# Splitting block 0's state product in a linear-attention plus gated-FFN kernel: two halves between gate and value of units 1 and 4, one decayed k on VectorE, plain idle products

## Chip, cores and metric

The kernel runs on one core of a Trainium2 chip. The metric is the device time of one execution in microseconds (us); lower is better. Kernels that are compared ran on the same chip in interleaved rounds. Engines are named as in the profile: PE is TensorE, DVE is VectorE ("Vector"), ACT is ScalarE ("Scalar"), POOL is GpSimd. PSUM, in the prediction, is where the kernel puts TensorE's results (its `psum()` tiles); XT is the attention output as the FFN reads it.

## The reference

Decayed linear attention over blocks, whose output goes through a gated FFN. Sizes: 4 batches, 8 heads, 768 positions, head dimension 64; FFN 512 to 1536 to 512.

```python
# for each block of positions, per head (lam is the decay of the head):
intra    = ((q @ k.T) * Dmask) @ v              # Dmask[i, j] = lam ** (i - j) for i >= j
inter    = (q * lam ** (pos + 1)) @ kv_state
out      = intra + inter
kv_state = lam ** block * kv_state + (k * lam ** (block - 1 - pos)).T @ v
# then, on x = out as (3072, 512):
y = (sigmoid(x @ w_gate) * (x @ w_val)) @ w_out
```

The kernel takes 128 positions at a time, so there are six blocks, numbered 0 to 5. "Decayed k" is the factor `k * lam ** (...)`; the "state product" is decayed k times v. A "unit" is a group of 128 of the 1536 FFN columns: four products of gate, a sigmoid on Scalar, four products of value, and one multiplication ("product") of the two on Vector.

## The kernel before

Weights and q, k, v are loaded by GpSimd's own DMA queue, so GpSimd spends time on issuing every load (0.76 to 1.17 us each in its timeline below), in program order with its arithmetic.

```python
WG, WV                                     # weights of gate and value, loaded in pieces:
def load_w(t, src, i, w):                  #   every load is issued by GpSimd
    nc.gpsimd.dma_start(out=t[:, :, fs], in_=src[:, :, fs])
# ...
zero = const.tile([128, 2 * C], FP32, tag="zero")           # C = 128
def idle(n):                                                # keeps TensorE busy while it waits
    for i in range(n):
        nc.tensor.matmul(wm[:, :2 * C], lhsT=zero[:, :C], rhs=zero, start=True, stop=True, ...)
# ...
def make_lamq():                                            # powers of lam for blocks 1 to 5
    lp = const.tile([128, HP, C], FP32, tag="lp")
    for u in range(2):
        us = slice(u * 64, (u + 1) * 64)
        nc.vector.tensor_copy(lp[us]..., lam_bc[us, :]...)              # 64 x 4, one input
    w = 1
    while w < C:                                                        # seven doublings, two inputs
        nc.vector.tensor_tensor(out=lp[:, :, w:2 * w], in0=lp[:, :, 0:w], in1=..., op=ALU.mult)
        w *= 2
    nc.vector.tensor_copy(lamq, lp)                                     # 128 x 512, one input
# ...
def make_kd(n):
    if n == 0:
        for bp in range(NB2):                               # two halves, two batches each
            nc.gpsimd.tensor_tensor(out=KD[n][:, bs], in0=K[n][:, bs], in1=kds..., op=ALU.mult)
        return
# ...
def c(n, *pairs):                                           # state product: 16 products per half,
    for bp in pairs:                                        # then Vector copies it to Sb
        ...
# ... order of the program around block 0:
piece_m(0, 3)                              # last mask product on Vector
# ...
prod(0, 0, v0)                             # unit 0
load_gv(3, GW)                             # GpSimd: issue two weight loads
make_kd(0)                                 # GpSimd: decayed k, both halves
load_gv(4, GW)                             # GpSimd: two weight loads
load(1, "qk", 0, 2)                        # GpSimd: q and k of block 1
# ...
gv(0, 1)                                   # unit 1: gate, sigmoid, value, product
make_lamq()
for ft in (2, 3): ...                      # gates 2 and 3
for ft in (2, 3): ...                      # values 2 and 3, products 2 and 3
gv(0, 4)                                   # unit 4
c(0, 0, 1)                                 # state product, both halves
# ...
gv(0, 5, 6, 7)
```

## Time and profile before

| | before |
|---|---|
| time, first three runs | 227.41 us median (227.41 to 227.60) |
| span that the profile records | 225.6 us |
| TensorE busy | 218.8 us, 97% |
| gate 1 / value 1 / gate 2 start | 16.95 / 18.32 / 19.34 us |
| value 4 / state product / gate 5 start | 24.00 / 24.96 / 25.59 us |

The engine table and the row of granted clock on the page of the kernel before (engine, busy us, share, instructions; one digit of the clock per fortieth of the span):

```profile
PE 218.8 (97%) x1746; PEld 117.5 (52%) x1768; DVE 104.2 (46%) x191; ACT 79.1 (35%) x149; POOL 80.8 (36%) x76
PEclk9999999999999999999999999999999999999999
```

TensorE is the engine that bounds the kernel. From 26 us to the end it is busy 195.5 of 199.6 us, and its products follow each other without holes that matter, so a gain has to come from the start. There the holes are few. The chain of waits of the kernel before (start us, us, what; it is the path that ended last):

```profile
11.18 7.09 DMA WV<-in_moe_w_val_dram
18.27 0.05 issue
18.32 1.04 PE vp L429 x4
19.35 3.63 PE gp L437 x16
...
23.28 0.68 DVE ht L450
23.96 0.04 issue
24.00 1.02 PE vp L429 x4
25.03 0.63 PE cp L407 x32
```

Value 1 waits for its weights, value 4 waits for Vector's product of unit 2, and the state product stands between value 4 and gate 5. Why Vector is late is seen in its timeline before (start us, us, engine, line, operation, out<-in, shape, count, and in brackets the idle time before it):

```profile
19.46 0.69 DVE L432 TENSOR_TENSOR ht<-sg,vp 128x512 bf16<-128x512 bf16 x1 [1.22 <-PE vp L429]
20.07 0.61 DVE L181 COPY lp<-lam_bc 64x4 f32<-64x4 f32 x2
20.71 1.85 DVE L185 TENSOR_TENSOR lp<-lp 128x4 f32<-128x4 f32 x7
22.60 0.77 DVE L188 CAST lamq<-lp 128x512 bf16<-128x512 f32 x1
23.28 1.26 DVE L450 TENSOR_TENSOR ht<-sg,gp 128x512 bf16<-128x512 bf16 x2
```

After the product of unit 1 (19.46) it builds lamq, and only then multiplies units 2 and 3. GpSimd's timeline before, over the same time:

```profile
16.70 3.77 POOL L361 TENSOR_TENSOR kd<-kb,kds 128x1024 bf16<-128x1024 bf16 x2
20.40 0.80 POOL L102 DMA_DIRECT2D WG<-in_moe_w_gate_dram  x1
21.20 0.76 POOL L102 DMA_DIRECT2D WV<-in_moe_w_val_dram  x1
21.94 1.17 POOL L85 DMA_DIRECT2D qb<-in_q_dram  x1
23.09 1.17 POOL L85 DMA_DIRECT2D kb<-in_k_dram  x1
```

The first of lamq's two copies took longer than its twin, as the view of that source line shows (minimum, median and maximum ns):

```profile
L181 DVE COPY lp<-lam_bc x2: 170/299/428, 20.1 to 20.5; 64x4 f32<-64x4 f32 x2
```

The long one ended at 20.50 us, just after GpSimd's decayed k (20.46).

### The profile page before, as it was taken

Reading aid. Unit: us, or ns where it says so; the run is one execution under the profiler, and the core shown is the slowest. Engines: PE = TensorE matmul, PEld = TensorE weight load, DVE = VectorE, ACT = ScalarE, POOL = GpSimd, SP = SyncE. Lnnn points to the kernel's source line nnn. Section 1 sums busy time; section 2 is a strip of 40 time slices with the busy share of each in tenths; the row PEclk is TensorE's granted clock in tenths of the full one; section 3 lists DMA queues with packets and bytes.
Section 4 is the critical chain, followed back from the end, with each engine's and each line's share of the span. In section 5 each row is a group of like instructions: output and inputs, shape, how many; then the busy total and the mean of one; then the engine's idle time right before and its main releaser. Section 6 shows DMA issues by size and latency. Waiting matters only on the chain.

```text
span 225.6 us, 4279 instructions
## 1 busy us (share of the span) xinstructions
PE 218.8 (97%) x1746; PEld 117.5 (52%) x1768; DVE 104.2 (46%) x191; ACT 79.1 (35%) x149; POOL 80.8 (36%) x76
## 2 busy tenths in 40 slices
PE   7989999999999999999999999999999999999994
PEld 5653455788864455444446444446444445444443
DVE  7866746586530522435642345742334850333300
ACT  5554234435422225333115333225333224433221
POOL 8999967973691007940005950000000000000000
PEclk9999999999999999999999999999999999999999
DMA  6999999999999991999021999921820012100022
GB/s 111 155 172 196 188 177 156 156 191 166 157 188 171 221 175 72 217 150 122 1 96 46 145 146 148 75 94 51 188 46 0 3 46 93 49 0 0 0 94 96
DMA packets 105860, 25.72 MB, mean 114 GB/s; under 512 B 95984, under 2 KB 102896, under 8 KB 105840
## 3 DMA queue, kind: packets, MB, share of 16 engines
q0 software_dynamic: 81232, 13.90, 79.7%
q1 hardware_dynamic: 23568, 11.28, 20.8%
q10 hardware_dynamic: 1040, 0.26, 0.5%
q8 instruction: 14, 0.23, 0.4%
q14 instruction: 6, 0.05, 0.1%
HBM read 28.32 MB, written 6.29 MB: 153 GB/s over the span
## 4 chain that ended last, share of the span: by engine, by line
PE 90%; POOL 4%; DMA 3%; issue 1%; DVE 0%; DVEq 0%; POOLq 0%
PE po L486 27%; PE vp L429 21%; PE gp L423 21%; PE gp L458 5%; PE vp L464 5%; DMA WV<-in_moe_w_val_dram 3%; PE sp L302 2%; PE gp L437 2%; PE op L314 2%; POOL vb L96 2%; PE op L326 1%; PE cp L407 1%; PE po L475 1%; POOL kb L96 1%; POOL qb L96 1%
## 5 line engine op out<-in xcount | busy, mean ns | idle before, releaser
L432 DVE TENSOR_TENSOR ht<-sg,vp 128x512 bf16<-128x512 bf16 x56 | 38.5, 687 | 66.8 <-PE vp L429 62.7
L486 PE MATMUL po<-WO,ht 128*128 128x512 bf16 x266 | 61.3, 379 | 0.5
L423 PE MATMUL gp<-XT,WG 128*128 128x512 bf16 x217 | 57.2, 379 | 0.6
L429 PE MATMUL vp<-XT,WV 128*128 128x512 bf16 x220 | 56.6, 379 | 0.5 <-DMA WV<-in_moe_w_val_dram 0.3
L426 ACT ACTIVATE sg<-gp 128x512 bf16<-128x512 f32 x56 | 33.4, 597 | 62.6 <-PE gp L423 62.6
L486 PEld LDWEIGHTS <-ht 128*128 128x128 bf16 x276 | 26.3, 98 | 31.0
L429 PEld LDWEIGHTS <-WV 128*128 128x128 bf16 x224 | 21.8, 98 | 27.4 <-DMA WV<-in_moe_w_val_dram 0.8
L423 PEld LDWEIGHTS <-WG 128*128 128x128 bf16 x224 | 21.4, 98 | 25.3
L489 ACT COPY ob<-po 128x512 f32<-128x512 f32 x23 | 13.5, 585 | 52.3 <-PE po L486 48.4
L199 DVE TENSOR_TENSOR MT<-sp,mask 128x512 bf16<-128x512 f32 x40 | 25.1, 682 | 10.3 <-PE sp L302 10.3
L388 POOL TENSOR_TENSOR sd<-Sb,dec 128x512 f32<-128x512 bf16 x8 | 8.1, 1035 | 43.8 <-DVE Sb L414 43.8
L458 PE MATMUL gp<-XT,WG 128*128 128x256 bf16 x96 | 14.4, 273 | 0.0
L464 PE MATMUL vp<-XT,WV 128*128 128x256 bf16 x96 | 14.4, 273 | 0.0
L468 DVE TENSOR_TENSOR ht<-sg,vp 128x256 bf16<-128x256 bf16 x24 | 10.0, 420 | 8.6 <-PE vp L464 8.6
L461 ACT ACTIVATE sg<-gp 128x256 bf16<-128x256 f32 x24 | 9.2, 383 | 13.0 <-PE gp L458 11.9
L96 POOL DMA_DIRECT2D vb<-in_v_dram x10 | 12.8, 1282 | 1.4 <-DMA kb<-in_k_dram 1.1
L379 POOL TENSOR_TENSOR kd<-kb,kds 128x1024 bf16<-128x1024 bf16 x6 | 11.3, 1903 | 3.1 <-DMA kb<-in_k_dram 3.1
L414 DVE TENSOR_TENSOR Sb<-cp,sd 128x512 bf16<-128x512 f32 x8 | 5.1, 686 | 15.5 <-PE cp L407 15.5
L341 ACT CAST XT<-op 128x512 bf16<-128x512 f32 x19 | 9.9, 598 | 2.1 <-PE op L314 2.0
L458 PEld LDWEIGHTS <-WG 128*128 128x128 bf16 x96 | 9.2, 98 | 1.7 <-issue 0.2
L464 PEld LDWEIGHTS <-WV 128*128 128x128 bf16 x96 | 9.4, 98 | 1.1
L217 PE MATMUL wm<-zero 128*128 128x256 f32 x20 | 8.4, 556 | 1.2 <-DVE ip L124 1.2
(83 smaller groups left out, 159.4 us busy)
## 6 DMA issues: line engine op xcount, KB each, us to landing
out_dram<-ob SPq DMA_DIRECT2D x21, 256.0 KB, 2.2
kb<-in_k_dram POOLq DMA_DIRECT2D x11, 256.0 KB, 10.2
qb<-in_q_dram POOLq DMA_DIRECT2D x9, 256.0 KB, 9.0
vb<-in_v_dram POOLq DMA_DIRECT2D x4, 512.0 KB, 14.1
WO<-in_moe_w_out_dram POOLq DMA_DIRECT2D x3, 512.0 KB, 8.5
WG<-in_moe_w_gate_dram POOLq DMA_DIRECT2D x5, 256.0 KB, 8.4
WV<-in_moe_w_val_dram POOLq DMA_DIRECT2D x5, 256.0 KB, 9.1
qb<-in_q_dram POOLq DMA_DIRECT2D x4, 128.0 KB, 8.3
```

What stands on the lines that cost most here:

```text
L96: nc.gpsimd.dma_start(out=lst[n][:, b0:b1], in_=src[b0:b1, :, sl, :].rearrange("b h s d -> s (b h) d"))
L199: nc.vector.tensor_tensor(out=out.rearrange("p (e x) c -> p e x c", e=2), in0=x.rearrange("p (e x) c -> p e x c", e=2), in1=mask.rearrange ...
L379: nc.gpsimd.tensor_tensor(out=KD[n][:, e], in0=K[n][:, e], in1=kds[:, e::2].unsqueeze(1).unsqueeze(3).to_broadcast([128, B, HP, D]), op=AL ...
L423: nc.tensor.matmul(gp, lhsT=WG[:, mt, fs], rhs=x[:, mt, :], start=(mt == 0), stop=(mt == NMT - 1))
L426: nc.scalar.activation(sg, gp, AF.Sigmoid)
L429: nc.tensor.matmul(vp, lhsT=WV[:, mt, fs], rhs=x[:, mt, :], start=(mt == 0), stop=(mt == NMT - 1))
L432: nc.vector.tensor_mul(HT[n, ft], sg, vp)
L458: nc.tensor.matmul(gp[:, cs], lhsT=WG[:, mt, fs], rhs=x[:, mt, cs], start=(mt == 0), stop=(mt == NMT - 1))
L464: nc.tensor.matmul(vp[:, cs], lhsT=WV[:, mt, fs], rhs=x[:, mt, cs], start=(mt == 0), stop=(mt == NMT - 1))
L468: nc.vector.tensor_mul(HT[n, ft][:, cs], sg[:, cs], vp[:, cs])
L486: nc.tensor.matmul(po, lhsT=HT[n, ft][:, tt * 128:(tt + 1) * 128], rhs=WO[:, ft, :], start=(ft == 0), stop=(ft == NFT - 1))
L489: nc.scalar.copy(ob, po)
```

## The change

The intent is to put half of the state product into the hole before value 1, so that less stands between value 4 and gate 5. For that, the first half of decayed k must be ready sooner, so it goes to Vector, which is idle then (1.25 us before 15.95 in the profile before). The idle products become bf16 of 512 columns in place of fp32 of 256. The diff, cut to its core:

```diff
-    zero = const.tile([128, 2 * C], FP32, tag="zero")
+    zero = const.tile([128, TCH], BF16, tag="zero")
...
-            nc.tensor.matmul(wm[:, :2 * C], lhsT=zero[:, :C], rhs=zero, start=True, stop=True,
+            nc.tensor.matmul(wm, lhsT=zero[:, :C], rhs=zero, start=True, stop=True,
...
+    def make_kd0(bp, eng):
+        ...                                      # one half, on the engine given
     def make_kd(n):
-        if n == 0:
-            ...                                  # both halves on GpSimd
...
-    idle(5)
+    idle(10)                                     # later counts: 1,1,1,1,1 -> 1,1,0,2,2
...
     piece_m(0, 3)
+    make_kd0(0, nc.vector)
...
     load_gv(3, GW)
-    make_kd(0)
+    make_kd0(1, nc.gpsimd)
     load_gv(4, GW)
...
-    gv(0, 1)
+    g1 = psum(); mm_part(g1, WG, 0, 1, 0, TCH); sigm(0, 1, g1)      # (joined into lines here)
+    c(0, 0)
+    v1 = psum(); mm_part(v1, WV, 0, 1, 0, TCH); prod(0, 1, v1)
     make_lamq()
...
-    gv(0, 4)
-    c(0, 0, 1)
+    g4 = psum(); mm_part(g4, WG, 0, 4, 0, TCH); sigm(0, 4, g4)
+    c(0, 1)
+    v4 = psum(); mm_part(v4, WV, 0, 4, 0, TCH); prod(0, 4, v4)
```

More of the change, by code (lines that the diff above doesn't have):

```diff
@@ L354, in piece_a0 @@
                 nc.scalar.copy(XT[0][:, m0:m0 + w, b, :], op)
-    def make_kd(n):
-        if n == 0:
-            KD[n] = kdp.tile([128, B, H, D], BF16, tag="kd", name="kd")
-            for bp in range(NB2):
-                bs = slice(2 * bp, 2 * bp + 2)
-                nc.gpsimd.tensor_tensor(
-                    out=KD[n][:, bs], in0=K[n][:, bs],
-                    in1=kds.unsqueeze(1).unsqueeze(3).to_broadcast([128, 2, H, D]), op=ALU.mult)
-            return
+    def make_kd0(bp, eng):
+        if bp == 0:
+            KD[0] = kdp.tile([128, B, H, D], BF16, tag="kd", name="kd")
+        bs = slice(2 * bp, 2 * bp + 2)
+        eng.tensor_tensor(out=KD[0][:, bs], in0=K[0][:, bs],
+                          in1=kds.unsqueeze(1).unsqueeze(3).to_broadcast([128, 2, H, D]), op=ALU.mult)
+    def make_kd(n):
         if n == 1:
@@ L515 @@
     piece_tq0([2])
-    idle(1)
     piece_tq0([3])
@@ L521 @@
     piece_m(0, 3)
+    make_kd0(0, nc.vector)
     piece_a0(0)
     piece_a0(1)
-    idle(1)
+    idle(2)
     piece_a0(2)
-    idle(1)
+    idle(2)
     g0 = psum()
@@ L564, in gvh @@
             piece_gvh(n, ft, i)
-    gv(0, 1)
+    g1 = psum()
+    mm_part(g1, WG, 0, 1, 0, TCH)
+    sigm(0, 1, g1)
+    c(0, 0)
+    v1 = psum()
+    mm_part(v1, WV, 0, 1, 0, TCH)
+    prod(0, 1, v1)
     make_lamq()
@@ L576 @@
         prod(0, ft, vp)
-    gv(0, 4)
-    c(0, 0, 1)
+    g4 = psum()
+    mm_part(g4, WG, 0, 4, 0, TCH)
+    sigm(0, 4, g4)
+    c(0, 1)
+    v4 = psum()
+    mm_part(v4, WV, 0, 4, 0, TCH)
+    prod(0, 4, v4)
     fade()
```

## The prediction

> **What bounds the kernel now.** The page's engine table has TensorE busy 218.8 of 225.6 us. In the timeline of PE, from 26 us to the end products follow each other at 0.216 us per 512 columns, apart from small gaps. The change touches nothing there, so only what happens before about 25.6 us can move the time. The chain there, gate 1, value 1, gates 2 and 3, values 2 and 3, gate 4, value 4, state product, gate 5, has three holes:
> - Value 1 starts at 18.32 us, 0.5 us after gate 1 stopped streaming (17.81), held by the load of its WV columns (chain of waits: DMA from 11.18 to 18.27).
> - Gate 2 starts at 19.34 us, 0.15 us late, behind its own load.
> - Value 4 starts at 24.00 us, 0.34 us after gate 4 stopped streaming; it waits for a PSUM buffer that the Vector product of unit 2 frees (waits view: "PE vp <- DVE ht"). Vector is late because it builds lamq first (20.07 to 23.28).
> Value 4 then ends at 24.87, the state product until 25.46, and gate 5 starts at 25.59.
>
> **What the change does.**
> 1. First half of the state product (16 products: 0.28 us by the trace, plus some 0.2 us at the changes of kind) goes to 17.9-18.3 us, into the hole before value 1. Free, with no slack; the hole before gate 2 gives 0.15 us more.
> 2. Its decayed k moves to Vector. The 512-wide mask product (same kinds of operand) repeats every 0.60 us; 1024 wide I estimate 1.13 us, 14.63 to 15.76. The next Vector instruction, the second half of XT for batch 3, started at 15.95. It fits.
> 3. GpSimd's decayed k ends at about 18.6 instead of 20.46. In the trace the first 64x4 copy of lamq took 428 ns, its twin 170 ns, and it ended 35 ns after the GpSimd product. [...] Without it the lamq chain gets 0.25 us shorter: unit 2's product starts at about 23.03, unit 3's ends at about 24.3.
> 4. Second half: takes the PSUM buffer freed by unit 2 (about 23.73), runs to about 24.05. Value 4 must now wait for unit 3's product, one buffer later: it starts at about 24.35. Gate 5 follows directly, at about 25.22 instead of 25.59.
> 5. Loads behind GpSimd are issued 1.9 us earlier; no product waits for them: worth nothing.
> 6. Idle products: ten of 512 columns at half clock need 4.27 us (before: 4.64), still ending before q's first cast (5.73). All lies in slack before 18.3 us, if the clock still rises near 7 us (the spacing of transposes fell from 107 to 56 ns there[...]).
>
> **Sum.** -0.37 us, all on the critical path: 227.41 to 227.05 us. Range 226.6 to 227.6. Chances: faster by over 2% 0.01, within 2% 0.98, slower 0.01.
>
> **Right or wrong in the profile.** Value 1 still at about 18.3; first lamq copy about 170 ns; value 4 at about 24.35, waiting for Vector; no state product after it; gate 5 near 25.2.
>
> **What would make it wrong.** [...]decayed k over 1.4 us on Vector, delaying XT and gate 1; the state's Vector copy pushing unit 1's product past 19.46; other landing times of the weights.

Clauses that no trace of this case shows are cut from it, in step 3, in step 6 and in the last paragraph, and likewise from some expectations below. -0.37 us is gate 5 at 25.22 in place of 25.59. "Without it" in step 3 means without GpSimd's decayed k beside lamq's first copy; the 0.25 us are about 428 less 170 ns.

## The result and the profile after

| | before | after |
|---|---|---|
| time | 227.41 us median of 6 (227.38 to 227.60) | 227.77 us median of 6 (227.05 to 228.10) |
| recorded spans (before: its 51 runs) | 225.6 to 225.8 us | 224.9 to 226.0 us |
| time minus span, mean of the same runs | 1.81 us | 2.12 us |

The ratio is 1.001, with a 95% interval of 0.9993 to 1.0027: within 2%. A ratio here is the mean time of one kernel's fast runs over that of the other's of the same rounds, so it is not quite the ratio of the medians that are quoted.

The predicted time was 227.05 us with a range to 227.6. The median lies 0.72 us above the forecast and outside the range. Two features were not in the forecast at all: the times of the change spread over a whole microsecond, while those of the kernel before keep within 0.4, and the part of the time that lies outside the recorded span grew by 0.3 us.

The page after, same lines as before:

```profile
PE 219.2 (97%) x1764; PEld 115.3 (51%) x1764; DVE 104.9 (47%) x192; ACT 79.2 (35%) x149; POOL 79.2 (35%) x75
PEclk9799999999999999999999999999999999999999
```

The second digit of the clock shows that in this execution the clock fell back once (the clock records give half speed from 8.58 to 12.00 us). In the same execution the first k load landed at 8.01 us, against 7.30 before. The chain of waits after begins with it:

```profile
1.26 6.75 DMA kb<-in_k_dram
...
18.78 0.37 PE cp L406 x16
19.16 5.29 PE gp L436 x24
24.44 0.37 PE cp L406 x16
24.81 0.98 PE gp L436 x4
```

And Vector's timeline after, the lines of lamq:

```profile
20.84 0.34 DVE L181 COPY lp<-lam_bc 64x4 f32<-64x4 f32 x2
21.21 1.85 DVE L185 TENSOR_TENSOR lp<-lp 128x4 f32<-128x4 f32 x7
23.09 0.43 DVE L188 CAST lamq<-lp 128x512 bf16<-128x512 f32 x1
```

From 17.76 us on this execution has no hole: gate 1, half a state product, value 1, gates, values, gate 4, the second half and value 4 follow each other, and the lamq copies are short. That is the intended picture, shifted by the late start: gate 1 began at 17.76 us against 16.95, and gate 5 at 25.63 against 25.59. So this one profile says "the change works, the loads were late". With six times between 227.05 and 228.10 one profile can't be the whole account.

### The profile page after: what moved, and what is told of

Same layout as the page of the kernel before. It is cut to its first block, busy times and chain, and to the rows that moved or that the text cites. A ratio compares the mean times of both kernels' runs of the same rounds, so it can differ in the third digit from the quotient of the medians.

```text
span 225.6 us, 4294 instructions
## 1 busy us (share of the span) xinstructions
PE 219.2 (97%) x1764; PEld 115.3 (51%) x1764; DVE 104.9 (47%) x192; ACT 79.2 (35%) x149; POOL 79.2 (35%) x75
## 4 chain that ended last, share of the span: by engine, by line
PE 94%; DMA 3%; DVE 1%; issue 0%; ACT 0%; POOLq 0%
PE po L485 27%; PE gp L422 21%; PE vp L428 21%; PE gp L457 5%; PE gp L436 5%; PE vp L463 5%; PE sp L302 3%; DMA kb<-in_k_dram 3%; PE op L314 3%; PE op L326 1%; PE cp L406 1%; PE po L474 1%; DVE MT L197 1%; PE tk L244 0%; ACT XT L354 0%
## 5 line engine op out<-in xcount | busy, mean ns | idle before, releaser
L431 DVE TENSOR_TENSOR ht<-sg,vp 128x512 bf16<-128x512 bf16 x54 | 37.2, 688 | 65.4 <-PE vp L428 65.4
L422 PE MATMUL gp<-XT,WG 128*128 128x512 bf16 x216 | 55.5, 379 | 0.0
L428 PE MATMUL vp<-XT,WV 128*128 128x512 bf16 x216 | 55.4, 379 | 0.0
L425 ACT ACTIVATE sg<-gp 128x512 bf16<-128x512 f32 x54 | 32.2, 597 | 59.5 <-PE gp L422 59.5
L428 PEld LDWEIGHTS <-WV 128*128 128x128 bf16 x216 | 21.2, 98 | 25.5
L422 PEld LDWEIGHTS <-WG 128*128 128x128 bf16 x216 | 20.7, 98 | 24.8
L457 PEld LDWEIGHTS <-WG 128*128 128x128 bf16 x96 | 9.2, 98 | 1.8 <-issue 0.2
L463 PEld LDWEIGHTS <-WV 128*128 128x128 bf16 x96 | 9.4, 98 | 1.1
L77 POOL DMA_DIRECT2D qb<-in_q_dram x8 | 9.4, 1182 | 0.0
```

Of the source, the lines that this page charges most:

```text
L422: nc.tensor.matmul(gp, lhsT=WG[:, mt, fs], rhs=x[:, mt, :], start=(mt == 0), stop=(mt == NMT - 1))
L425: nc.scalar.activation(sg, gp, AF.Sigmoid)
L428: nc.tensor.matmul(vp, lhsT=WV[:, mt, fs], rhs=x[:, mt, :], start=(mt == 0), stop=(mt == NMT - 1))
L431: nc.vector.tensor_mul(HT[n, ft], sg, vp)
L457: nc.tensor.matmul(gp[:, cs], lhsT=WG[:, mt, fs], rhs=x[:, mt, cs], start=(mt == 0), stop=(mt == NMT - 1))
L463: nc.tensor.matmul(vp[:, cs], lhsT=WV[:, mt, fs], rhs=x[:, mt, cs], start=(mt == 0), stop=(mt == NMT - 1))
```

## The experiments

Theories, with the letters that the texts use:
- **L**, load issues: with less work on GpSimd, its issue of the q load moves about 1.9 us forward, from 21.94 to about 20.1 us, and lies across lamq's small copies, which it holds up.
- **C**, clock: with the new idle products the clock rises or falls at other times, and this spreads the times.
- **D**, arrival of data: the landing times of loads vary from execution to execution whatever the kernel, so the old kernel should spread too.
- **N**, length of Vector's program: the 0.3 us outside the span come with the number of instructions that Vector has in the built program. Before it is 311, after it is 313 (the traces hold 309 and 311 Vector records, the same two more): the two more belong to the decayed k on Vector.

All runs in one table. "Outside" is time minus recorded span, mean of the runs; the ratio is against the kernel before in the same rounds.

| run | what it is | Vector instr. | median us (range) | ratio, 95% interval | outside us |
|---|---|---|---|---|---|
| before_again | the kernel before | 311 | 227.41 (227.37–227.53) | 0.9998, 0.9986–1.0010 | 1.77 |
| after_again | the change | 313 | 227.80 (227.14–228.08) | 1.0009, 0.9996–1.0022 | 2.12 |
| after_third | the change | 313 | 227.79 (227.17–228.16) | 1.0010, 0.9998–1.0021 | 2.10 |
| chain_only | change, old idle products | 313 | 227.58 (227.13–227.84) | 1.0001, 0.9988–1.0014 | 2.11 |
| idle_only | before, new idle products | 311 | 227.36 (227.34–227.78) | 0.9999, 0.9987–1.0011 | 1.77 |
| kd_only | before, half of decayed k on Vector | 313 | 227.53 (227.32–228.04) | 1.0010, 0.9998–1.0023 | 2.16 |
| c_only | change, all decayed k on GpSimd | 311 | 227.67 (227.59–227.71) | 1.0010, 0.9998–1.0022 | 1.87 |
| tt_copy | change, lamq's copies with two inputs | 313 | 227.21 (227.16–227.70) | 0.9997, 0.9983–1.0010 | 2.10 |
| pool_late | change, GpSimd kept busy as before | 313 | 227.75 (227.65–227.78) | 1.0014, 1.0002–1.0027 | 2.13 |
| lamq_late | tt_copy, lamq's cast after unit 4 | 313 | 227.29 (227.14–227.52) | 0.9996, 0.9984–1.0009 | 2.16 |
| tt_all | change, copies and cast with two inputs | 313 | 227.17 (227.10–227.79) | 0.9996, 0.9984–1.0009 | 2.13 |
| before_tt | before, lamq's copies with two inputs | 311 | 227.38 (227.36–227.54) | 0.9999, 0.9987–1.0011 | 1.81 |
| before_tt2 | before, copies and cast with two inputs | 311 | 227.31 (227.29–227.41) | 0.9995, 0.9983–1.0007 | 1.79 |
| dve_plus | before, one dead memset on Vector | 312 | 228.60 (228.56–228.63) | 1.0051, 1.0039–1.0063 | 2.07 |
| dve_two | before, two dead memsets on Vector | 313 | 228.62 (228.61–228.68) | 1.0053, 1.0040–1.0066 | 2.13 |
| after_minus | change, one Vector instruction fewer | 312 | 228.15 (227.72–228.67) | 1.0029, 1.0016–1.0042 | 2.01 |
| lamq_late_minus | lamq_late, one Vector instruction fewer | 312 | 228.01 (227.69–228.60) | 1.0027, 1.0015–1.0039 | 2.03 |
| lamq_act | change, lamq's copies on Scalar, cast late | 311 | 227.00 (226.90–227.09) | 0.9981, 0.9967–0.9994 | 1.84 |

All outputs are right. Most of these differences are smaller than their intervals, so the argument rests on the profiles, on how wide each kernel spreads, and on the split of the time into span and rest.

### Is the spread the change's own? before_again, after_again, after_third

No edit: the two kernels again.

> The old kernel once more, for a second profile. Ratio 1.000, times 227.4 to 227.6. Theory C: whatever its loads do, the clock rises near 7 us and stays up. Theory D: if the loads land at 8.0 us in this profile, its time must rise by 0.5 us or so; if k never lands later than 7.3 us in this kernel, then the late loads belong to the change.

> The change as it is, once more, for a second profile and for its spread. Theory C (clock: [...]the clock falls back to half speed for 3.4 us between 8.6 and 12 us, and the first stage runs late): the times spread again over about 1 us, from 227.0 to 228.1, and whether the clock in the trace falls back decides where the profiled run lies. Theory D (loads: the first loads simply landed 0.7 us late in the profiled run, by chance): the profiled run has k at either 7.3 or 8.0 us and gate 5 moves with it, and the old kernel, whose loads vary as much, shows the same spread.

> The change as it is, for a third profile. Theory L: in the three groups of times, 227.1, 227.8 and 228.1, the first copy or the cast of lamq tells them apart: near 228.1 a copy is held (784 ns in the second profile), near 227.1 none is and the loads are early; times 227.0 to 228.1 with a median of 227.6 to 227.9.

The kernel before gave 227.37 to 227.53. The change fell again into groups. Its 18 runs in all are 227.05, .14, .15, .17, .30, .31; then 227.74, .78, .79, .80, .80, .80, .81; then 228.05, .08, .09, .10, .16. Their mean is 227.67 us. All 51 runs of the kernel before lie between 227.33 and 227.69. So D does not hold as put: the arrival of data alone doesn't spread the old kernel.

The profile of after_again fell in the slowest group (228.08 us). Its first k load landed at 7.33 us, as before, and its clock did not fall back. Vector's timeline in after_again:

```profile
20.55 0.96 DVE L181 COPY lp<-lam_bc 64x4 f32<-64x4 f32 x2
21.55 1.85 DVE L185 TENSOR_TENSOR lp<-lp 128x4 f32<-128x4 f32 x7
23.43 0.43 DVE L188 CAST lamq<-lp 128x512 bf16<-128x512 f32 x1
23.78 1.28 DVE L449 TENSOR_TENSOR ht<-sg,gp 128x512 bf16<-128x512 bf16 x2
```

GpSimd's timeline in after_again:

```profile
16.70 1.91 POOL L360 TENSOR_TENSOR kd<-kb,kds 128x1024 bf16<-128x1024 bf16 x1
...
20.18 1.16 POOL L85 DMA_DIRECT2D qb<-in_q_dram  x1
```

TensorE's timeline in after_again:

```profile
17.85 0.44 PE L406 MATMUL cp<-vb,kd 128*64 128x64 bf16 x16
18.80 1.04 PE L436 MATMUL gp<-XT,WV 128*128 128x512 bf16 x3 [0.51 <-DMA WV<-in_moe_w_val_dram]
...
24.51 0.44 PE L406 MATMUL cp<-vb,kd 128*64 128x64 bf16 x16 [0.36 <-DVE ht L449]
25.11 1.02 PE L436 MATMUL gp<-XT,WV 128*128 128x512 bf16 x4 [0.15 <-DVE ht L449]
```

The first copy took 784 ns (20.55 to 21.33) and ended when the issue of the q load ended (21.34). Here TensorE does wait for Vector, and value 4 starts at 25.11 us in place of the predicted 24.35, gate 5 at 25.97. Gate 5 decides the span: in 19 of the 20 profiles the span is 200.0 to 200.1 us longer than its start (200.6 in lamq_late_minus, which no run explains). The profile of after_third (227.81 us, the middle group) has the same wait in a smaller form: value 1 at 18.54, first copy at 20.29 in 154 ns, second copy 785 ns (20.46 to 21.24, with the issue from 20.08 to 21.25), value 4 at 24.83.

### Which part of the change? idle_only, chain_only, kd_only, c_only

idle_only is the old kernel with the new `zero`, `idle` and counts. chain_only is the rest of the change with the old ones.

> The old kernel with only the new idle products. Theory C: slower than before and spread out, 227.4 to 228.5, median about 227.9 (ratio 1.002 or more), with the clock falling back in the slow ones. Theory D: as before, 227.4 to 227.6, ratio 1.000.

> The change with the old fp32 idle products at their five old places; decayed k and the two halves of the state product as in the change. Theory C: the clock stays up from 7 us, the spread goes, and the gain that I forecast appears: 227.05 (ratio 0.9984), value 1 at 18.3, gate 5 near 25.2 us. Theory D: as the changed kernel, 227.0 to 228.1, with a spread of 1 us.

idle_only is the kernel before: 227.36 us, copies and cast as before (195 and 775 ns in its profile), gate 5 at 25.58. One of its five runs, 227.78 us with a span of 226.0, lies above every run of the kernel before and stays unexplained. Chain_only spreads like the change (227.13 to 227.84). So the idle products are not the cause, and C falls. The clock records agree: the clock rose at 7.00 us in the first profile of the kernel before and at 5.70 in before_again, with the same gate 5 (25.59 and 25.58). Chain_only's profile happened to have a late first load again (k at 7.94 us), as the first profile of the change had.

kd_only takes one part of the rest: only the engine of decayed k's first half.

```diff
     piece_m(0, 3)
+    make_kd0(0, nc.vector)
...
-    make_kd(0)
+    make_kd0(1, nc.gpsimd)
```

> The old kernel with only the first half of the decayed k on Vector: old idle products, the state product in one piece after value 4. Theory L: GpSimd's load issues move onto lamq here too, so the times spread to 228 although the state product stays where it was: 227.1 to 228.1. My forecast would have had it 0.25 us faster, 227.15. If the state product in the holes is what costs, this one stays at 227.15 to 227.5 with no spread.

It spreads from 227.32 to 228.04 us. Vector's and then GpSimd's timeline in kd_only:

```profile
20.14 1.09 DVE L181 COPY lp<-lam_bc 64x4 f32<-64x4 f32 x2
```

```profile
20.07 1.17 POOL L85 DMA_DIRECT2D qb<-in_q_dram  x1
```

The second copy took 920 ns (20.31 to 21.23), against an issue that ended at 21.24. So moving the decayed k is enough to bring the hold and the spread, without any new place for the state product.

c_only is the counterpart: both halves of decayed k stay on GpSimd.

```diff
-    make_kd0(0, nc.vector)
...
     load_gv(3, GW)
+    make_kd0(0, nc.gpsimd)
     make_kd0(1, nc.gpsimd)
```

> The change with both halves of the decayed k on GpSimd, at the old place: only the state product in two halves and the new idle products are left. Vector has as many instructions as in the old kernel. Theory N: time minus span 1.8. In the span: the load issues stand at the old times, so the copy is held until 20.5 us and lamq ends near 23.3; value 4 waits for unit 3's product until about 24.6, gate 5 about 25.45: times 227.2 to 227.5 in a narrow band. Theory P gives the same here: this run settles the state product's own share.

The spread is gone (227.59 to 227.71) and the time outside the span is back at 1.87 us, but the median, 227.67, missed its expectation of 227.2 to 227.5. TensorE's timeline in c_only says why:

```profile
18.65 0.44 PE L406 MATMUL cp<-vb,kd 128*64 128x64 bf16 x16 [0.77 <-POOL kd L360]
```

The first half waits for GpSimd, value 1 comes only at 19.03 us, and the gain is used up. The decayed k on Vector is needed for the first half to fit in its hole; this part of the change's design is right. In c_only a copy was held as well, by another load: 392 ns from 20.78 to 21.17, across the WG issue that ended at 21.20.

### Is it the load issue that holds the copies? tt_copy, pool_late

L is tested by writing the same copy in another form, with two inputs in place of one, as the maximum of a value with itself. That a load issue would not hold this form was the assumption; no run had tested it before:

```diff
-            nc.vector.tensor_copy(lp[us]..., lam_bc[us, :]...)
+            nc.vector.tensor_tensor(out=lp[us]..., in0=src, in1=src, op=ALU.max)   # src = lam_bc[us, :]...
```

> The change, with the two 64x4 copies that begin lamq written as the maximum of a value with itself: a Vector instruction with two inputs instead of one. Theory L ([...]these copies are held until GpSimd has finished issuing q's load, which the change moved from 21.9 to 20.2 us, onto the start of lamq): both take about 170 ns in every run, gate 5 comes up to 0.6 us sooner when the loads are early, and the times near 228.1 vanish: highest about 227.85, median about 227.5. Theory F (only the landing of value 1's weights, 18.3 to 18.8 us, spreads the times): nothing changes, 227.1 to 228.1, median 227.8.

Vector's timeline in tt_copy, then GpSimd's and TensorE's:

```profile
20.30 0.33 DVE L182 TENSOR_TENSOR lp<-lam_bc 64x4 f32<-64x4 f32 x2
```

```profile
20.07 1.17 POOL L85 DMA_DIRECT2D qb<-in_q_dram  x1
```

```profile
24.22 1.02 PE L437 MATMUL gp<-XT,WV 128*128 128x512 bf16 x4
25.08 1.03 PE L423 MATMUL gp<-XT,WG 128*128 128x512 bf16 x4
```

GpSimd's issue of the q load ran from 20.07 to 21.24 us in this profile, so the two instructions lie inside it and took 151 and 163 ns. The second, which began 0.39 us into the issue, is the test: in after_third a one-input copy that began 0.38 us into it took 785 ns. (The first began 0.22 us into it, and one-input copies that began so early ran free too, in after_third and in the first profile of the change; one that began 0.24 us into it was held, 920 ns in kd_only.) Value 1 was at 18.55 us, as in after_third, yet gate 5 came at 25.08 in place of 25.69. Four of five runs were 227.16 to 227.26 (one 227.70); the group at 228.1 did not appear. The mean span fell to 225.20 us, against 225.56 for the change: the hold cost 0.36 us on average. Of the 15 runs of the three versions of the change with two-input copies and unmoved tiles (tt_copy, lamq_late, tt_all) 13 have a span of 225.3 us or less, against 6 of the 18 of the change. The two others (227.70 and 227.79, span 225.6) were not profiled, so the hold is not the only thing that can put a run in the middle group.

The ends fit as well. Take from the end of each instruction that an issue held the time that it takes when free (154 to 170 ns for a copy, 427 for the cast): in all twelve profiles with such a hold it then starts 0.16 to 0.19 us before the recorded end of the issue. That is why the cast of the kernel before runs on 0.25 us past the issue.

pool_late goes the other way. The change stays whole, but GpSimd computes the first half once more into a dead tile, so that its load issues come at the old times:

```diff
+    kdx = const.tile([128, 2, H, D], BF16, tag="kdx", name="kdx")
+    nc.gpsimd.tensor_tensor(out=kdx, in0=K[0][:, 0:2], in1=kds..., op=ALU.mult)
     make_kd0(1, nc.gpsimd)
```

> The change, with GpSimd doing the first half of the decayed k once more, into a tile that nobody reads: Vector's part and the state product stay as in the change, but GpSimd issues the later loads at the old times (20.4 us on). Theory L: GpSimd's extra work makes the kernel steadier and no slower: the first copy is held until 20.46 us again (some 400 ns), lamq ends near 23.3, value 4 starts near 24.6, times 227.2 to 227.6, median about 227.35. Theory F: as the change, 227.1 to 228.1, median 227.8, for the loads of the weights up to unit 5 are issued before this.

The spread shrank to 0.13 us, as L says. The level did not go where it was expected: 227.75, with a span of 225.5 to 225.7. With the issues at their old times the copies are free (156 ns) but the cast is held again (620 ns), and outside the span it has the 2.13 us of the change in place of 1.81.

### Does the old kernel have the hold as well? before_tt, before_tt2

Step 3 of the prediction expected 0.25 us from a lamq chain that is no longer held at its first copy. before_tt tests that alone: the kernel before, with the same edit as tt_copy.

> The old kernel with only the two 64x4 copies of lamq as a maximum (two inputs). Theory L[...]: the first copy falls from 428 to about 160 ns, but the chain reaches lamq's cast 0.25 us sooner, while GpSimd issues q's load (21.9 to 23.1 us), and the cast is held until 23.1 us as before: lamq ends near 23.28 again, times as before, 227.35 to 227.6. My forecast's step 3 (taking the hold off the first copy makes lamq 0.25 us shorter) would give 227.15.

Vector's timeline in before_tt:

```profile
20.31 0.35 DVE L182 TENSOR_TENSOR lp<-lam_bc 64x4 f32<-64x4 f32 x2
...
22.57 0.78 DVE L189 CAST lamq<-lp 128x512 bf16<-128x512 f32 x1
23.27 1.26 DVE L451 TENSOR_TENSOR ht<-sg,gp 128x512 bf16<-128x512 bf16 x2
```

In this profile value 1 happened to come at 18.56 us in place of 18.32, so the copies started at 20.31 and took 172 and 164 ns. They ended at 20.66 us, only 0.02 before those of the kernel before (20.68), so lamq reached its cast no sooner: the run is no test of what 0.25 us off the copies is worth. idle_only, with the one-input copies and value 1 at 18.54, has the same times (copies 195 and 168 ns to 20.67). The product of unit 2 started at 23.27, as before (23.28).

This shows the likely reason that the old kernel is so steady. Whether value 1 comes at 18.32 or at 18.56 us, the copies end at 20.66 to 20.68, just after GpSimd's decayed k (20.45 to 20.46), and the cast ends at 23.35 to 23.36, set by the q issue. By these figures a cast that came 0.25 us sooner would have been held to the same end; that is worked out, no run shows it. pool_late, with the old issue times, has little spread too.

before_tt2 gives the cast two inputs as well.

> The old kernel with all three one-input copies of lamq, the cast too, as a maximum; nothing else of the change. Theory L: no hold is left, the cast takes about 0.65 us and lamq ends near 22.95 instead of 23.28; value 4 follows gate 4 at about 23.7; gate 5 near 25.28; times 227.05 to 227.25, without the change. [...]

It was 227.31 us, against 227.05 to 227.25 expected. The cast took 691 ns, its full two-input time (tt_all has the same 691), so the load issue no longer held it. But the two-input first copy was held until GpSimd's decayed k ended at 20.46 us: it took 408 ns. So the edit of before_tt and before_tt2 does not take the first hold away, and "no hold is left" was wrong. So in these profiles either form is held by something: the one-input copy by a load issue (784 ns in after_again) and by GpSimd's arithmetic (428 ns before), the two-input copy by the arithmetic (408 ns here), but not by the issue that it met in tt_copy (163 ns).

### The change without any hold: lamq_late, tt_all

lamq_late is tt_copy with lamq's cast moved behind the product of unit 4; tt_all is the change with all three one-input instructions of lamq given two.

> The copies as a maximum, and lamq's last cast put after unit 4's product, so that the products of units 2 and 3 no longer wait for it. Theory L: Vector no longer holds the state product's second half and value 4; Tensor streams from gate 2 to gate 5 without a hole: gate 5 at about 25.0 to 25.5 us, times 226.8 to 227.6, median about 227.2. Theory F: gate 5 moves only with value 1, median about 227.6 or more.

> The change with all three copies of lamq as a maximum. Theory L: as the run with the two copies alone, for there the cast (427 ns) was not held; 0.2 us longer at most[...]: median 227.2 to 227.4, highest about 227.8. Were the cast held in the slower runs (those at 227.7), they would come down too: highest 227.4.

Medians 227.29 and 227.17 us, mean spans 225.16 and 225.20. In both profiles the weights of value 1 landed early (17.02 and 17.06 us), value 1 began at 18.20 and 18.23, right behind the half state product, and the copies started at 19.95 and 19.97, before the q issue (20.09 and 20.10); the second ones began 0.02 and 0.04 us into it. Gate 5 came at 25.00 and 25.05 us, sooner than the 25.22 of the prediction. The chain itself was therefore not overrated. (The highest run of tt_all, 227.79, passed the 227.4 that was expected if a held cast made the slow runs; so a held cast does not explain it.)

### What is outside the span? dve_plus, dve_two, after_minus, lamq_late_minus

N was tested by adding dead instructions to the old kernel and taking one from the change.

```diff
+    dead = const.tile([128, 1], FP32, tag="dead", name="dead")      # dve_plus, in the kernel before
+    nc.vector.memset(dead, 0.0)
```

```diff
+    dead = const.tile([128, 16], FP32, tag="dead", name="dead")     # dve_two, in the kernel before
+    for i in range(2):
+        nc.vector.memset(dead[:, i:i + 1], 0.0)
```

```diff
-    p1 = const.tile([128, 1], FP32, tag="p1")                       # the two *_minus kernels
-    for lo in range(0, 128, 32):
-        nc.vector.tensor_scalar_add(p1[lo:lo + 32], loc[lo:lo + 32, 0:1], float(lo))
+    p1 = loc[:, 0:1]
+    nc.vector.tensor_scalar_add(p1[64:128], p1[64:128], 64.0)
+    nc.vector.tensor_scalar_add(p1[32:64], p1[32:64], 32.0)
+    nc.vector.tensor_scalar_add(p1[96:128], p1[96:128], 32.0)
```

> The old kernel with one dead instruction on Vector among the constants: a memset of one column that nobody reads. Theory N (one more instruction in Vector's program costs a fixed third of a microsecond outside the recorded span): span 225.6 as before, time minus span 2.1 instead of 1.8, times 227.65 to 227.9. Theory P (the extra goes with where the decayed k is computed): span and time as before, 227.35 to 227.6.

> The change with one Vector instruction less among the constants (the partition index built by three additions in place instead of four): as many as the old kernel. Theory N: time minus span falls to 1.8 and all times by 0.33 us: 226.7 to 227.8, median about 227.45. Theory P: time minus span stays 2.1, times 227.05 to 228.15, median 227.8.

> The kernel with lamq's copies as a maximum and its cast moved back, with one Vector instruction less. Theory N: 0.33 us below lamq_late: times 226.8 to 227.2, median about 226.95, faster than both kernels in every run (ratio about 0.998). Theory P: 227.1 to 227.5 as lamq_late.

> The old kernel with two dead memsets of one column on Vector, into a new 64-byte tile, so that all other tiles keep their place modulo 64 bytes. Theory N (the length of Vector's program): span 225.6 as before, first loads at 7.3 and 9.0 us as before, time minus span 2.1 instead of 1.8: times 227.65 to 227.9. If the extra went with computing the decayed k on Vector: time minus span 1.8, times 227.35 to 227.6.

For the time outside the span N held in direction, not in size. One dead memset gave 2.07 us, two gave 2.13, against 1.77 to 1.81 of the kernel before; a fixed third of a microsecond for each instruction it is not. The two kernels with one instruction fewer were expected at 1.8 because the change was taken to have one more than the kernel before. It has two, so they stand at 312, and the time outside fell by only 0.10 and 0.13 us, to 2.01 and 2.03. Over all kernels the values are 1.77 to 1.87 at 311 instructions, 2.01 to 2.07 at 312 and 2.10 to 2.16 at 313. The trace has no record outside the span, so the mechanism stays open; shown is only that the added time goes with the number of Vector's instructions. That dead ones do it rests on kernels whose tiles moved as well (below); but c_only and lamq_act, with the tiles unmoved, are back at 311 and at 1.87 and 1.84 us.

The four totals missed, for a reason that no theory had. In all four the first loads were slower: 0.90 us per 128 KB (in dve_plus they landed at 9.74, 10.64 and 11.55 us), against 0.83 (9.03, 9.85, 10.69 before). All that follows was later, and the old kernel's span grew to 226.5 us. These are exactly the four kernels in which the edit moved later tiles in SBUF by 32 or 64 bytes. dve_two, whose tile was made 64 bytes so that addresses stay multiples of 64, was slow all the same. The association with the moved tiles is all that was tested. pool_late narrows it: its extra tile moves the later ones by 2048 bytes, and its loads keep their pace (9.09, 9.93, 10.77 us). The kernels place block 0's q tile at byte 68352 in the kernel before and 70400 in pool_late, and at 68320, 68384 and 68416 in the four. What it is about the place that goes with slower loads, no run shows. In after_minus, too, the granted clock was 0.991 to 0.992 in five of six runs, and in lamq_late_minus 0.992 in two of five; of the 18 runs of the change only the first has this. The totals of the four, then, say nothing about N; only the split into span and rest does.

### A version with neither cost: lamq_act

If N and L are both right, a version of the change with 311 Vector instructions and no one-input copy in the way should come near the predicted time. lamq's two copies go to Scalar, early, and the cast goes behind unit 4's product.

```diff
+    lp = const.tile([128, HP, C], FP32, tag="lp")
+    for u in range(2):
+        us = slice(u * 64, (u + 1) * 64)
+        nc.scalar.copy(lp[us]..., lam_bc[us, :]...)
...
     def make_lamq():
-        ...                                       # the tile and the two copies on Vector
-        nc.vector.tensor_copy(lamq, lp)
...
     prod(0, 4, v4)
+    nc.vector.tensor_copy(lamq, lp)
```

> The change with lamq's two first copies made early by Scalar, which is idle there, and lamq's cast moved behind unit 4's product: no Vector copy in the path of value 4, and Vector's program as long as in the old kernel. Tiles keep their addresses modulo 64 bytes. Theory N with theory L: time minus span 1.8, span 224.9 to 225.3 (up to 225.7 when the first loads land late), times 226.75 to 227.5, median about 226.95, ratio to the old kernel 0.998. Without N: as lamq_late, 227.1 to 227.5.

The median is 227.00 us, range 226.90 to 227.09, ratio 0.9981 with an interval of 0.9967 to 0.9994: faster than the kernel before, by little, and steady. Time minus span is 1.84 us, span 225.1. Vector's timeline in lamq_act (the doublings of lamq follow unit 1's product at once), then TensorE's:

```profile
19.54 0.69 DVE L448 TENSOR_TENSOR ht<-sg,gp 128x512 bf16<-128x512 bf16 x1 [0.34 <-PE gp L435]
20.14 1.84 DVE L185 TENSOR_TENSOR lp<-lp 128x4 f32<-128x4 f32 x7
```

```profile
24.20 1.04 PE L435 MATMUL gp<-XT,WV 128*128 128x512 bf16 x4
25.07 1.03 PE L421 MATMUL gp<-XT,WG 128*128 128x512 bf16 x4
```

## Why the prediction was wrong

It said 227.05 us by a sum of one term, -0.37, inside the span. The 18 runs of the change have a mean of 227.67, against 227.44 for the kernel before. The +0.23 between the means is +0.30 outside the span (2.11 against 1.81) and -0.06 inside it (225.56 against 225.62), rounded. The median stands 0.1 us above the mean, because the fast group has a third of the runs.

- **Not in the sum at all: +0.30 us outside the span.** The forecast took the time to move as the chain inside the span moves. It goes with Vector's program being two instructions longer: dve_two has as much with two dead ones (2.13 us), though with moved tiles, and lamq_act and c_only show that it goes when they go (1.84 and 1.87 us). Why is open.
- **Step 5 failed: "Loads issued 1.9 us earlier; no product waits for them: worth nothing."** The loads' landings were indeed worth nothing: from gate 5 to the end the profiles take 200.0 us before and after. Their issue was not. On GpSimd the q load's issue moved from 21.94 to 20.1 us, onto lamq's copies, and held one of them for about 0.6 to 0.75 us. kd_only shows it with this part alone, tt_copy shows it gone, and pool_late shows the spread gone with the old issue times. On average it is worth 0.36 us of span (225.56 against 225.20 in tt_copy), nearly as much as the whole predicted gain.
- **Step 3 failed: "Without it the lamq chain gets 0.25 us shorter".** The reading was right that GpSimd's decayed k held the first copy (428 ns against 170). But lamq was not free without it. In the change (after_again) the q issue holds the copies instead, 0.96 against 0.61 us, which is 0.35 us lost, and that eats the 0.34 us that the cast, now free, gives back. The prediction had also missed the hold on the cast in the kernel before (0.77 us in place of 0.43). With it the 0.25 us would have been lost there too; that is worked out from the times, for before_tt, which was to show it, does not test it.
- **Step 1 was right in kind, and its "Value 1 still at about 18.3" missed.** The half state product did sit in the hole (17.85 us in after_again) and cost nothing. But the weights of value 1 landed either at 17.0 to 17.7 us or at 18.3 to 18.8 us (leaving out dve_plus and dve_two with their slow loads); the kernel before and its other variants showed only the late landing. In 13 of the 20 profiles the landing came 2.0 to 2.1 us after the start of a 16 KB instruction fetch that the DMA records show near 16.2 to 17.1 us (before: 16.18 and 18.27; after_again: 16.72 and 18.76); in the other seven the load was through at most 0.8 us after that start, and the next load landed only 2.4 to 2.8 us after it. That the fetch delays one load is the guess from this order; no run moved the fetch alone, so it isn't shown.
- **How the pieces make groups.** If value 1 starts at 18.80, lamq's first copy meets the q issue (after_again, 228.08 us). If it starts at 18.54, the first copy gets through and the second is held (after_third, 227.81). If it starts at 18.2, the first is done before the issue begins and the second starts at most 0.04 us into it, as in the profiles of lamq_late and tt_all (there with two inputs); this fits the group at 227.1, but no profile of the change itself fell into that group, so it is argued, not shown. The first profile of the change is of the middle group by another road: late first loads moved everything, and the copies started just 0.05 us into the issue and were free. So a middle time has at least two roads, and how many of the unprofiled runs took which is not known.
- **Step 2 was right.** Decayed k took 1.21 to 1.22 us on Vector (forecast 1.13) and did not delay the XT copy (15.89 us in after_again, 15.95 before).
- **Step 4 was right in kind.** Value 4 waits for the product of unit 3 where Vector is late (25.11 us in after_again, for a product of Vector). Without the hold it starts at 24.2 us, a little better than the forecast 24.35.
- **Step 6 was right in effect.** idle_only equals the kernel before in four of five runs. That the clock rises near 7 us was the luck of one profile: it rose at 5.70 us in before_again and at 3.87 us in c_only. The clock did fall back in one profile of the change (and in those of the two kernels with one Vector instruction fewer, which also had late first loads), but that execution of the change, 227.74 us, was no slower than its group.

The total is closed by lamq_act. Without the hold and without the two Vector instructions the same state product in two halves gives 227.00 us; the prediction was 227.05. That they are so near is partly luck: lamq_act also has the copies and the cast of lamq out of the path of value 4, which the prediction did not count on, and its value 4 waits for nothing. What stays open: why Vector's program length shows outside the span; why two of the profiles of kernels with the new chain had first loads 0.7 us late, and whether that was chance; and the 0.90 us per load in the four kernels with moved tiles.

## What to carry to other kernels

When work leaves an engine that also issues DMA, its issues come sooner (here 20.1 in place of 21.94 us): look at what the other engines run at the new times, because, as here, the issue itself can hold an instruction even where no one waits for the load (784 to 920 ns for copies that take 154 to 170). When a wait is taken away, look for the next wait behind it before booking the gain (here the load issue behind GpSimd's arithmetic), and be wary of a kernel that is very steady (227.33 to 227.69 us in 51 runs here), since something fixed may be setting its pace. And split every measured time into the recorded span and the rest before explaining a difference of a few tenths of a microsecond, and repeat the profile when the times fall in groups.
